# A retention layer followed by a low-rank mixer: stores moved to the GpSimd queue, and casts, transposes and scores placed as three separate steps

## The chip, the cores and the metric

The kernel runs on one core of one Trainium2 chip. The metric is the device time of a run in microseconds (us); of several runs the median counts. A core has five engines that run their own instruction streams in order and meet through semaphores: TensorE (PE in the profile, with PEld for its weight loads), VectorE (DVE), ScalarE (ACT), GpSimd (POOL) and SyncE (SP). A transfer is started by an instruction in the stream of one of these engines ("SPq", "ACTq" are the queues) and carried by 16 shared DMA engines.

## The reference

Four sequences (B = 4) of S = 768 tokens go through two layers. The first is a retention layer with H = 8 heads of D = 64: the state decays by a constant gamma of the head at each token and takes in the outer product of key and value, and the query reads it.

```python
for t in range(S):
    state = gamma * state + einsum('bhd,bhe->bhde', k[:, :, t], v[:, :, t])
    y[:, :, t] = scale * einsum('bhd,bhde->bhe', q[:, :, t], state)
```

Its output, laid out as x of shape (4, 768, 512), goes through a mixer: a low-rank mix over the tokens (rank 32), then a feed-forward part with 2048 hidden columns. Inputs and output are float32.

```python
h = xt @ U @ V                     # xt: x with tokens last
u = x + h.transpose(0, 2, 1)
out = u + maximum(u @ w_ch1, 0) @ w_ch2
```

## The kernel before

**Tiling.** A sequence is cut into six chunks of 128 tokens; two chunks make a block, so there are three blocks a sequence. In a chunk the retention is done in its parallel form: scores (key times query, masked to the causal half), a running state, and a mix of both into x.

**Steps of one block, and their lines.** `prep_block(b, bk)` (L205) is GpSimd work: it turns the loaded float32 tiles into bf16, `qTi` (L211, with the decay of the query), `kTi` (L215), and for each of the two chunks `kd` (L220) and `vd` (L225, with the decay of the key). After every one of these six casts it calls `feed_one` (L106), which puts the next load of a fixed list into SyncE's stream. `turn_block` (L327) makes VectorE transpose `qTi` and `kTi` in four instructions (L334). `score4(b, ci)` (L337) is the TensorE work of a chunk on the transposed tiles (L345), the causal mask on VectorE (L350), and the update of the state on TensorE (L363, which reads `kd` and `vd`), taken out of PSUM by ScalarE. `mix4` (L372) ends the chunk on TensorE (L382, L388), and ScalarE copies x out. When all six chunks are done, `lr_proj`, `lr_expand` and `lr_turn` (L400 to L431) do the low-rank mix and transpose its result u.

**The feed-forward part.** `mlp_pieces(b)` (L442) cuts it into 32 pieces "up" (16 with 512 columns, 16 with 256; four matmuls each on L451, then a Relu, every third on VectorE at L456 and the others on ScalarE at L458) and 24 pieces "down" (four matmuls each on L474; after each fourth piece VectorE adds u to the result in `o_sb`, L479, and a store of 256 KB is put on a list). Three buffers hold `o_sb`, so the add of the fourth tile needs the first store to have landed.

**What sets the order.** All streams are written by hand. `weave` (L488) writes the pieces of sequence b-1 one after the other, and between them, at given fractions of their total cost, the steps of sequence b: these are the marks, numbers in the tables `AT` (five for each block: begin, score, mix, score, mix) and `LR`. `store()` (L437) writes the next store of the list into ScalarE's stream, one piece after its add. In the table of before the first of the five marks of a block does both `prep_block` and `turn_block`. There are four weaves: in the first three the pieces of sequences 0, 1 and 2 run with the retention of sequences 1, 2 and 3 between them, and the fourth has the pieces of sequence 3 alone. Sequence 0's retention comes ahead of them, by a loop of its own, while the weights are loaded and cast.

**Buffers that the steps touch.** `rblk` has two buffers for each of `qTi`, `kTi` and the transposed `qT`, `kT`; `rpre` has four each for `kd` and `vd`, that is two blocks' worth; `rin2` has four for the loads of q and k in block form, again two blocks' worth; `rin` has 19 for all other loads. Each transfer that SyncE or ScalarE starts takes one of eight completion semaphores (DMAHW0 to DMAHW7), and waits until that semaphore's transfer before it has landed.

Of the kernel before, what the change touches and what calls it, by code (L numbers as in the profile page):

```python
# [17 lines left out]
def kernel(  # L18
# [11 lines left out]
    nc = tc.nc  # L30
    P = 128
    B, H, S, D = q.shape
# [73 lines left out]
    def feed_one():  # L106
        if n_fed[0] == len(feed):
            return
        key, src = feed[n_fed[0]]
        n_fed[0] += 1  # L110
        if key[0] == "uv":
            nc.sync.dma_start(out=Uf,
                              in_=moe_U.rearrange("(j p) r -> p j r", p=P))
            for c in range(NCB):
                nc.sync.dma_start(out=Vf[ds(RK * c, RK)], in_=moe_V)
            return
        if key[0] in ("qT", "kT"):
            t = rin2.tile([P, 1024], fp32, tag="in2", name=f"in2_{n_fed[0]}")
            ready[key] = t
            for hp in range(4):  # L120
                nc.sync.dma_start(
                    out=t[ds(32 * hp, 32)].rearrange("p (h x) -> p h x", h=2),
                    in_=src[ds(2 * hp, 2)].rearrange("h (t j) d -> t h (j d)",
                                                     t=32))
            return
        t = rin.tile([P, 512], fp32, tag="in", name=f"in_{n_fed[0]}")
        ready[key] = t
        if key[0] in "qkv":
            t = t.rearrange("p (h d) -> p h d", h=H)
        nc.sync.dma_start(out=t, in_=src)  # L130

    def take(*key):
        assert feed[n_used[0]][0] == key, (feed[n_used[0]][0], key)
        n_used[0] += 1
        return ready.pop(key, None)
# [69 lines left out]
    def prep_block(b, bk):  # L205
        for nm in ("qT", "kT"):
            src = take(nm, b, bk).rearrange("p (a j d) -> p a j d", a=8, j=2)
            t = rblk.tile([P, 8, D, 2], bf16, tag=nm + "i", name=f"{nm}i_{b}_{bk}")
            dst = t.rearrange("p a d j -> p a j d")
            if nm == "qT":  # L210
                nc.gpsimd.tensor_tensor(  # L211
                    dst, src, gqT[:, bk, :, :, None].to_broadcast([P, 8, 2, D]),
                    op=ALU.mult)
            else:
                nc.gpsimd.tensor_copy(out=dst, in_=src)  # L215
            pre[nm, b, bk] = t
            feed_one()
        for ci in (2 * bk, 2 * bk + 1):
            t = rpre.tile([P, H, D], bf16, tag="kd", name=f"kd_{b}_{ci}")
            nc.gpsimd.tensor_copy(  # L220
                out=t, in_=take("k", b, ci).rearrange("p (h d) -> p h d", h=H))
            pre["k", b, ci] = t
            feed_one()
            t = rpre.tile([P, H, D], bf16, tag="vd", name=f"vd_{b}_{ci}")
            nc.gpsimd.tensor_tensor(  # L225
                t, take("v", b, ci).rearrange("p (h d) -> p h d", h=H),
                gk[:, ci, :, None].to_broadcast([P, H, D]), op=ALU.mult)
            pre["v", b, ci] = t
            feed_one()
# [97 lines left out]
    def turn_block(b, bk):  # L327
        for nm in ("qT", "kT"):
            src = pre.pop((nm, b, bk)).bitcast(fp32).rearrange(
                "p (h j) (c w) o -> p h j c (w o)", h=2, c=2)  # L330
            t = rblk.tile([P, 2, 2, 256], bf16, tag=nm, name=f"{nm}_{b}_{bk}")
            dst = t.bitcast(fp32).rearrange("p h c (t j) -> p h j c t", j=4)
            for i in range(2):
                nc.vector.transpose(out=dst[:, i], in_=src[:, i])  # L334
            bts[nm, b, bk] = t
# [60 lines left out]
    def lr_open(b):  # L396
        us[b] = xp.tile([P, NCK, DM], bf16, tag="u", name=f"u_{b}")
        uTs[b] = xp.tile([P, NCB, S], bf16, tag="uT", name=f"uT_{b}")

    def lr_proj(b):  # L400
        for j in range(NCK):
            for c in range(NCB):
                nc.tensor.matmul(R[ds(RK * c, RK), 3, :P], Ub[:, j],  # L403
                                 xs[b][:, j, ts(c, P)], start=(j == 0),
                                 stop=(j == NCK - 1))
        pcs[b] = rmid.tile([P, P], bf16, tag="pc", name=f"pc_{b}")
        evac("D", pcs[b], R[:, 3, :P])
# [29 lines left out]
    def store():  # L437
        if stores:
            dst, src = stores.pop(0)
            nc.scalar.dma_start(out=dst, in_=src)  # L440

    def mlp_pieces(b):  # L442
        gT = gtp.tile([P, NM, S], bf16, tag="gT", name=f"gT_{b}")
# [44 lines left out]
    def weave(pieces, marks):  # L488
        total = sum(c for c, _ in pieces)
        marks = sorted(((total * at, f) for at, f in marks), key=lambda m: m[0])  # L490
        at = 0.0
        for cost, f in pieces:
            while marks and marks[0][0] <= at:
                marks.pop(0)[1]()
            late = len(stores)
            f()
            if late:
                store()
            at += cost
        for _, f in marks:  # L500
            f()
        while stores:
            store()

    def part(f, *args):
        return lambda: f(*args)
# [39 lines left out]
    for j in range(4):  # L546
        prep_w2(j)

    AT = {1: ((0.30, 0.33, 0.39, 0.43, 0.49), (0.62, 0.64, 0.69, 0.72, 0.77),
              (0.79, 0.81, 0.85, 0.87, 0.91)),  # L550
          2: ((0.12, 0.14, 0.20, 0.24, 0.30), (0.33, 0.35, 0.41, 0.45, 0.51),
              (0.54, 0.56, 0.62, 0.66, 0.72))}
    AT[3] = AT[2]
    LR = {1: (0.94, 0.96, 0.98, 0.99), 2: (0.76, 0.80, 0.88, 0.92)}
    LR[3] = LR[2]
    for b in range(1, B):
        if b > 1:
            marks = [(0.02, part(lr_expand, b - 1, 4, 2)),
                     (0.07, part(lr_turn, b - 1, 4))]
        else:  # L560
            marks = [(0.03, part(lr_expand, 0, 4, 2)), (0.10, part(lr_turn, 0, 4)),
                     (0.16, part(lr_expand, 0, 0, 4))]
        for bk in range(NBK):
            def begin(bk=bk):
                if (b, bk) != (1, 0):
                    prep_block(b, bk)
                turn_block(b, bk)
            ci = 2 * bk
            marks += zip(AT[b][bk], (begin, part(score4, b, ci), part(mix4, b, ci),
                                     part(score4, b, ci + 1),  # L570
                                     part(mix4, b, ci + 1)))

        def mixed():
            lr_open(b)
            lr_proj(b)
        marks += zip(LR[b], (mixed, part(lr_expand, b, 0, 4), part(lr_turn, b, 0),
                             part(lr_turn, b, 2)))
        weave(mlp_pieces(b - 1), marks)
    b = B - 1
# [32 lines left out]
```

## Time and profile before

| what | us |
|---|---|
| median of 3 runs (lowest to highest) | 267.06 (266.52 to 267.25) |
| the profiled execution, its own time | 268.16 |
| its span, first to last instruction | 266.3 |
| TensorE busy in the span | 226.4 |
| VectorE, ScalarE, GpSimd busy | 105.7, 84.0, 96.8 |
| mean granted TensorE clock | 0.974 |

The profiled execution's own time is 1.86 us longer than its span, and 1.10 us over the median. All views are of this execution, in us from the span's start. "Busy" of TensorE comes from modelled ends of its matmuls; what it lacks to the length of a stretch is time in which it waited.

### The profile page before, as it was taken

What the parts mean: (1) busy time and instruction counts of PE and PEld (TensorE: products, weight loads), DVE (VectorE), ACT (ScalarE), POOL (GpSimd) and SP (SyncE); (2) the same over time, 40 slices, a digit from 0 to 9 for tenths busy, and PEclk for the clock granted to TensorE, in tenths of its full rate; (3) what the DMA queues carried; (4) which work ended last, traced back from release to release, by engine and by line L of the source; (5) the groups of instructions that cost most, each with busy time, mean ns of one, the idle gap of its engine ahead of it and who ended that gap; (6) DMA issues with size and microseconds to landing.
All of it is one profiled execution on the core that took longest, in us unless ns stands there. A gap on an engine that the chain in (4) does not pass through costs nothing.

```text
span 266.3 us, 5538 instructions
## 1 busy us (share of the span) xinstructions
PE 226.4 (85%) x2284; PEld 123.8 (47%) x2284; DVE 105.7 (40%) x188; ACT 84.0 (32%) x159; POOL 96.8 (36%) x125
## 2 busy tenths in 40 slices
PE   1565557997997599497999999979999999999994
PEld 1344443445643234243575445435754454475441
DVE  3132212356352614236656333466563334232211
ACT  2533323444501010343553003435530034452000
POOL 4786584886503655455520242456000000000000
PEclk9999999999999859689999999999999999999999
DMA  8999899999319879599900675696002121000222
GB/s 165 218 218 192 271 382 194 279 380 234 76 50 260 206 195 237 142 190 219 221 6 2 153 210 172 163 240 116 0 5 81 42 79 39 0 2 0 79 81 79
DMA packets 70986, 39.14 MB, mean 147 GB/s; under 512 B 59056, under 2 KB 59056, under 8 KB 70960
## 3 DMA queue, kind: packets, MB, share of 16 engines
q1 hardware_dynamic: 67504, 32.48, 54.1%
q10 hardware_dynamic: 3456, 6.29, 6.4%
q8 instruction: 18, 0.29, 0.5%
q14 instruction: 8, 0.07, 0.1%
HBM read 32.47 MB, written 6.29 MB: 146 GB/s over the span
## 4 chain that ended last, share of the span: by engine, by line
PE 72%; DVE 6%; DMA 4%; ACT 2%; issue 1%; SPq 0%; POOL 0%; POOLq 0%; ACTq 0%; DVEq 0%
PE mlp L451 31%; PE mlp L474 30%; PE r L428 2%; PE r L345 2%; DMA in<-in_v_dram 2%; DVE qT L334 2%; DMA out_dram<-o 2%; PE r L388 2%; DVE kT L334 2%; DVE gT L456 1%; PE st L363 1%; ACT uT L76 1%; PE r L382 1%; PE r L412 1%; PE r L403 1%
## 5 line engine op out<-in xcount | busy, mean ns | idle before, releaser
L451 PE MATMUL mlp<-uT,w1b 128*128 128x512 bf16 (+1 forms) x512 | 92.0, 334 | 1.8 <-ACT uT L76 1.8
L474 PE MATMUL mlp<-w2b,gT 128*128 128x512 bf16 x384 | 90.5, 386 | 0.0
L451 PEld LDWEIGHTS <-w1b 128*128 128x128 bf16 x512 | 48.9, 99 | 34.8 <-issue 6.3
L458 ACT ACTIVATE gT<-mlp 128x512 bf16<-128x512 f32 (+1 forms) x88 | 42.8, 490 | 44.6 <-PE mlp L451 37.9
L474 PEld LDWEIGHTS <-gT 128*128 128x128 bf16 x384 | 36.0, 99 | 40.3 <-issue 2.2
L456 DVE TENSOR_SCALAR gT<-mlp 128x512 bf16<-128x512 f32 (+1 forms) x40 | 22.2, 555 | 39.9 <-PE mlp L451 39.9
L479 DVE TENSOR_TENSOR o<-mlp,u 128x512 f32<-128x512 f32 x24 | 16.5, 689 | 48.9 <-PE mlp L474 48.9
L350 DVE TENSOR_TENSOR a<-r,mask 128x512 bf16<-128x512 f32 x36 | 23.2, 685 | 15.3 <-PE r L345 9.9
L76 ACT ACTIVATE x<-r 128x512 bf16<-128x512 f32 x24 | 14.3, 596 | 38.5 <-PE r L388 32.4
L225 POOL TENSOR_TENSOR vd<-in,gk 128x512 bf16<-128x512 f32 x18 | 18.8, 1042 | 13.9 <-DMA in<-in_v_dram 8.9
L215 POOL CAST kTi<-in 128x1024 bf16<-128x1024 f32 x9 | 12.0, 1329 | 29.4 <-DMA in<-in_k_dram 25.5
L211 POOL TENSOR_TENSOR qTi<-in,gqT 128x1024 bf16<-128x1024 f32 x9 | 17.1, 1904 | 13.4 <-DMA in<-in_q_dram 9.3
L419 DVE TENSOR_TENSOR u<-r,x 128x512 bf16<-128x512 f32 (+1 forms) x16 | 14.6, 953 | 15.8 <-PE r L412 15.8
L303 DVE TENSOR_TENSOR a<-r,mask 128x512 bf16<-128x512 f32 x12 | 7.7, 686 | 26.2 <-ACT x L76 13.9
L76 ACT ACTIVATE uT<-r 128x1024 bf16<-128x1024 bf16 x10 | 10.2, 1021 | 24.9 <-PE r L428 24.9
L220 POOL CAST kd<-in 128x512 bf16<-128x512 f32 x18 | 11.0, 612 | 15.7 <-DMA in<-in_k_dram 15.2
L76 ACT ACTIVATE ns<-st 128x256 bf16<-128x256 f32 x15 | 5.7, 383 | 27.7 <-PE st L363 27.7
L345 PE MATMUL r<-qT,kT 32*128 32x128 bf16 x288 | 8.4, 218 | 6.3 <-DVE kT L334 6.3
L271 PE MATMUL r<-ident,qd 128*128 128x128 bf16 x24 | 3.5, 302 | 10.6 <-POOL qd L238 5.1
L76 ACT ACTIVATE qkT<-r 128x1024 bf16<-128x1024 bf16 x6 | 6.1, 1023 | 17.2 <-PE r L273 17.2
L252 POOL CAST w1b<-in 128x512 bf16<-128x512 f32 x16 | 9.8, 613 | 4.6 <-DMA in<-in_moe_w_ch_dram 4.0
L345 PEld LDWEIGHTS <-kT 32*128 32x128 bf16 x288 | 4.2, 92 | 14.3 <-DVE kT L334 10.2
(63 smaller groups left out, 148.5 us busy)
## 6 DMA issues: line engine op xcount, KB each, us to landing
in<-in_moe_w_ch_dram SPq DMA_DIRECT2D x32, 256.0 KB, 5.5
in<-in_k_dram SPq DMA_DIRECT2D x24, 256.0 KB, 5.0
in<-in_v_dram SPq DMA_DIRECT2D x24, 256.0 KB, 5.1
out_dram<-o ACTq DMA_DIRECT2D x24, 256.0 KB, 2.0
in<-in_q_dram SPq DMA_DIRECT2D x36, 128.0 KB, 4.7
in<-in_k_dram SPq DMA_DIRECT2D x36, 128.0 KB, 3.7
in<-in_q_dram SPq DMA_DIRECT2D x6, 256.0 KB, 5.1
Vf<-in_moe_V_dram SPq DMA_DIRECT2D x4, 96.0 KB, 3.9
```

The source lines that it names most:

```text
L76: nc.scalar.activation(dst, src, AF.Copy)
L211: nc.gpsimd.tensor_tensor(dst, src, gqT[:, bk, :, :, None].to_broadcast([P, 8, 2, D]), op=ALU.mult)
L215: nc.gpsimd.tensor_copy(out=dst, in_=src)
L225: nc.gpsimd.tensor_tensor(t, take("v", b, ci).rearrange("p (h d) -> p h d", h=H), gk[:, ci, :, None].to_broadcast([P, H, D]), op=ALU.mult)
L345: nc.tensor.matmul(R[:, hp, ts(i, P)], kT[r, i, c, tok], qT[r, i, c, tok], start=(c == 0), stop=(c == 1))
L350: nc.vector.tensor_tensor(a[:, ds(4 * g, 4)].rearrange("p (n i) m -> p n i m", n=2), R[:, ds(2 * g, 2), :256].rearrange("p n (i m) -> p n ...
L419: nc.vector.tensor_tensor(v4(us[b][:, ds(j0, nj), e]), R[:, ds(2 * g, 2), :nj * P].rearrange("p c (j e) -> p c j e", j=nj), v4(xs[b][:, ds ...
L451: nc.tensor.matmul(g_p[:, :sz], w1b[:, c, ts(m, P)], uTs[b][:, c, ds(lo, sz)], start=(c == 0), stop=(c == NCB - 1))
L456: nc.vector.tensor_relu(gT[:, m, ds(lo, sz)], g_p[:, :sz])
L458: nc.scalar.activation(gT[:, m, ds(lo, sz)], g_p[:, :sz], AF.Relu)
L474: nc.tensor.matmul(ch, gT[:, m, ts(j, P)], w2b[:, m], start=(m == 0), stop=(m == NM - 1))
L479: nc.vector.tensor_tensor(o_sb, ch, us[b][:, j], op=ALU.add)
```

## The change

Three things are edited.

1. `store()` issues the transfer from GpSimd's stream instead of ScalarE's.
2. `prep_block` is no longer part of a block's first mark. The casts of sequence 1's second block are written ahead of the first weave; the third block's casts of each sequence come right after the fifth mark of its first block, and the casts of the next sequence's first two blocks after the fifth marks of the second and third block. So every cast stands one block earlier than it did.
3. The marks are new numbers. A block's first mark, now the transposes alone, stands 0.05 to 0.07 of the pieces' cost ahead of the first score, where it was 0.02 or 0.03; and `lr_turn` moves from 0.07 to 0.06 in the second and third weave.

```diff
     def store():
         if stores:
             dst, src = stores.pop(0)
-            nc.scalar.dma_start(out=dst, in_=src)
+            nc.gpsimd.dma_start(out=dst, in_=src)
...
-    AT = {1: ((0.30, 0.33, 0.39, 0.43, 0.49), (0.62, 0.64, 0.69, 0.72, 0.77),
-              (0.79, 0.81, 0.85, 0.87, 0.91)),
+    prep_block(1, 1)
+
+    AT = {1: ((0.27, 0.32, 0.38, 0.42, 0.48), (0.56, 0.62, 0.67, 0.71, 0.76),
+              (0.74, 0.80, 0.84, 0.87, 0.91)),
...
-                     (0.07, part(lr_turn, b - 1, 4))]
+                     (0.06, part(lr_turn, b - 1, 4))]
...
-            def begin(bk=bk):
-                if (b, bk) != (1, 0):
-                    prep_block(b, bk)
-                turn_block(b, bk)
             ci = 2 * bk
-            marks += zip(AT[b][bk], (begin, part(score4, b, ci), part(mix4, b, ci),
-                                     part(score4, b, ci + 1),
+            marks += zip(AT[b][bk], (part(turn_block, b, bk), part(score4, b, ci),
+                                     part(mix4, b, ci), part(score4, b, ci + 1),
                                      part(mix4, b, ci + 1)))
+        marks.append((AT[b][0][4] + 0.005, part(prep_block, b, 2)))
+        if b + 1 < B:
+            marks.append((AT[b][1][4] + 0.005, part(prep_block, b + 1, 0)))
+            marks.append((AT[b][2][4] + 0.005, part(prep_block, b + 1, 1)))
```

**SyncE, the loads of sequence 1's second block.** The last four loads of that block (in_646 and in_649 are k and v of its second chunk) and what each waits for; DMAHW is the completion semaphore that it takes, Pool a buffer that GpSimd must have freed. Ahead of the change ScalarE's first store, of o_0, waits for and takes DMAHW6 too.

```order
-L130 DMA in_640<-in_k_dram 128x8x64 [waits DMAHW4_49,Pool_49]
-L130 DMA in_643<-in_v_dram 128x8x64 [waits DMAHW5_49,Pool_49]
-L130 DMA in_646<-in_k_dram 128x8x64 [waits DMAHW6_49,Pool_49]
-L130 DMA in_649<-in_v_dram 128x8x64 [waits DMAHW7_49,Pool_49]
+L130 DMA in_640<-in_k_dram 128x8x64 [waits DMAHW3_49,Pool_49]
+L130 DMA in_643<-in_v_dram 128x8x64 [waits DMAHW4_49,Pool_49]
+L130 DMA in_646<-in_k_dram 128x8x64 [waits DMAHW5_49,Pool_49]
+L130 DMA in_649<-in_v_dram 128x8x64 [waits DMAHW6_49,Pool_49]
```

With the stores gone from these eight semaphores, loads alone take them, strictly in turn, and each load waits for the load that stands eight ahead of it.

**GpSimd, the first weave.** What now stands between the casts of sequence 1's third block and those of sequence 2's first block; DMAHW are loads, PE buffers that TensorE must have read, and DVE in a store's row is the add that fills o_0, o_1 or o_2.

```order
L220 CAST kd_4_1086<-in_664 128x512 [waits DMAHW7_49,PE_49,Pool_49]
L225 TENSOR_TENSOR vd_4_1090<-in_667,gk 128x512 [waits DMAHW0_49,PE_49,Pool_49]
L220 CAST kd_5_1094<-in_670 128x512 [waits DMAHW1_49,PE_49,Pool_49]
L225 TENSOR_TENSOR vd_5_1098<-in_673,gk 128x512 [waits DMAHW2_49,PE_49,Pool_49]
L440 DMA out_dram<-o_0_1134 128x512 [waits DVE_49]
L440 DMA out_dram<-o_1_1191 128x512 [waits DVE_49]
L440 DMA out_dram<-o_2_1273 128x512 [waits DVE_49]
L211 TENSOR_TENSOR qTi_0_1312<-in_70_676,gqT 128x8x2x64 [waits DMAHW5_49,DMAHW4_49,DMAHW6_49,DMAHW3_49,Pool_49]
```

Before there were casts alone in this stream; now the first three stores stand behind the last cast of the third block, and the next block's casts behind the stores.

**VectorE, start of the second weave.** Before, from the first Relus (L456; mlp is a PSUM bank) to the mask of the first chunk's scores (L350):

```order
L456 TENSOR_SCALAR gT_1537<-mlp_1560 128x512
L456 TENSOR_SCALAR gT_1537<-mlp_1587 128x512
L334 STREAM_TRANSPOSE qT_0_1623<-qTi_0_1593 128x4x64 x2
L334 STREAM_TRANSPOSE kT_0_1626<-kTi_0_1600 128x4x64 x2
L350 TENSOR_TENSOR a_2_0_1651<-r,mask 128x512 x2
```

And with the change, the same stretch:

```order
L456 TENSOR_SCALAR gT_1597<-mlp_1620 128x512
L334 STREAM_TRANSPOSE qT_0_1641<-qTi_0_1312 128x4x64 x2
L334 STREAM_TRANSPOSE kT_0_1644<-kTi_0_1319 128x4x64 x2
L456 TENSOR_SCALAR gT_1597<-mlp_1653 128x512
L350 TENSOR_TENSOR a_2_0_1681<-r,mask 128x512 x2
```

The four transposes moved ahead of the second Relu, which follows a matmul group three pieces later in TensorE's stream.

More of the change, by code (lines that the diff above doesn't have):

```diff
@@ L547 @@
         prep_w2(j)
-    AT = {1: ((0.30, 0.33, 0.39, 0.43, 0.49), (0.62, 0.64, 0.69, 0.72, 0.77),
-              (0.79, 0.81, 0.85, 0.87, 0.91)),
-          2: ((0.12, 0.14, 0.20, 0.24, 0.30), (0.33, 0.35, 0.41, 0.45, 0.51),
-              (0.54, 0.56, 0.62, 0.66, 0.72))}
+    prep_block(1, 1)
+    AT = {1: ((0.27, 0.32, 0.38, 0.42, 0.48), (0.56, 0.62, 0.67, 0.71, 0.76),
+              (0.74, 0.80, 0.84, 0.87, 0.91)),
+          2: ((0.08, 0.13, 0.19, 0.23, 0.29), (0.27, 0.34, 0.40, 0.44, 0.50),
+              (0.48, 0.55, 0.61, 0.65, 0.71))}
     AT[3] = AT[2]
```

## The prediction

> **What bounds it now.** The first rows are from the page: the busy line, and the shares of the chain that ended last.
>
> ```profile
> PE 226.4 (85%) x2284; PEld 123.8 (47%) x2284; DVE 105.7 (40%) x188; ACT 84.0 (32%) x159; POOL 96.8 (36%) x125
> PE 72%; DVE 6%; DMA 4%; ACT 2%; issue 1%; SPq 0%; POOL 0%; POOLq 0%; ACTq 0%; DVEq 0%
> ```
>
> TensorE bounds the kernel and nothing else comes near, so a change gains only what TensorE loses by waiting or by a low clock. Next I cut the span into its weaves: the chain in order of time (start, length, what) has the first matmuls of each.
>
> ```profile
> 43.90 3.57 PE mlp L451 x8
> 111.64 1.87 PE mlp L451 x4
> 166.90 0.86 PE mlp L451 x4
> 220.13 0.86 PE mlp L451 x4
> ```
>
> The three weaves that carry retention work take 67.7, 55.3 and 53.2 us for nearly the same matmuls, so the losses sit in the first. The view of windows finds them (length, then busy us of PE, PEld, DVE, ACT, POOL; granted clock; DMA share; GB/s).
>
> ```profile
> 58.00:62.00 4.00, 2.77 (x13) 1.08 (x11) 2.10 (x6) 1.79 (x3) 3.50 (x6) 1.00 1.05 339
> 62.00:66.00 4.00, 3.68 (x65) 3.08 (x66) 2.60 (x6) 1.64 (x5) 1.82 (x4) 1.00 0.84 201
> 70.00:74.00 4.00, 4.00 (x47) 2.37 (x46) 0.74 (x2) 1.60 (x4) 0.81 (x1) 1.00 0.02 4
> 94.00:96.00 2.00, 2.00 (x6) 0.74 (x5) 0.69 (x1) 0.00 (x0) 0.79 (x1) 0.50 1.03 243
> 120.00:122.00 2.00, 0.62 (x11) 0.12 (x9) 2.00 (x5) 0.60 (x1) 1.09 (x2) 1.00 1.07 227
> 122.00:124.00 2.00, 1.83 (x38) 0.90 (x31) 1.53 (x3) 0.52 (x2) 0.85 (x1) 1.00 1.06 227
> 170.00:180.00 10.00, 8.46 (x82) 4.12 (x80) 5.13 (x9) 4.76 (x9) 4.95 (x5) 1.00 0.93 221
> ```
>
> At each first block TensorE stands still for 1.5 us; near 95 us it is busy at half clock; and at 70 to 74 us the DMA engines carry nothing (share 0.02). The timeline of TensorE shows what the pauses between 82 and 94 us waited for (in brackets), and those of SyncE and ScalarE why.
>
> ```profile
> 85.09 0.30 PE L363 MATMUL st<-vd,kd 128*32 128x64 bf16 x16 [1.98 <-POOL vd L225]
> 90.68 0.29 PE L345 MATMUL r<-qT,kT 32*128 32x128 bf16 x8 [1.16 <-DVE kT L334]
> 91.14 0.29 PE L345 MATMUL r<-qT,kT 32*128 32x128 bf16 x8 [0.17 <-DVE kT L334]
> 92.99 0.41 PE L363 MATMUL st<-vd,kd 128*32 128x64 bf16 x16 [1.56 <-POOL vd L225]
> 65.48 0.53 SPq L130 DMA_DIRECT2D in<-in_v_dram  x1
> 78.31 0.37 SPq L130 DMA_DIRECT2D in<-in_k_dram  x1
> 76.19 0.37 ACTq L440 DMA_DIRECT2D out_dram<-o  x1
> ```
>
> SyncE issues a load of v at 65.48 and nothing more until 78.31, 2.1 us after ScalarE issued the first store: that k load takes the semaphore which the store had. From there everything is late: loads, GpSimd's casts, VectorE's transposes, TensorE.
>
> **The change part by part.** *Stores off the eight semaphores, casts a block early.* SyncE's next load no longer waits for a store, so it can go at 66.0 instead of 78.3: the third block's loads, and with them its casts, move up by 12.3 us. GpSimd's timeline has those casts, the page their means.
>
> ```profile
> 81.49 0.61 POOL L220 CAST kd<-in 128x512 bf16<-128x512 f32 x1 [10.67 <-DMA in<-in_k_dram]
> 91.89 1.04 POOL L225 TENSOR_TENSOR vd<-in,gk 128x512 bf16<-128x512 f32 x1 [1.42 <-DMA in<-in_v_dram]
> 93.75 1.04 POOL L225 TENSOR_TENSOR vd<-in,gk 128x512 bf16<-128x512 f32 x1
> L211 POOL TENSOR_TENSOR qTi<-in,gqT 128x1024 bf16<-128x1024 f32 x9 | 17.1, 1904 | 13.4 <-DMA in<-in_q_dram 9.3
> L215 POOL CAST kTi<-in 128x1024 bf16<-128x1024 f32 x9 | 12.0, 1329 | 29.4 <-DMA in<-in_k_dram 25.5
> ```
>
> The chunk whose `vd` came at 91.89 then has it at 79.6 to 80.6; TensorE reaches it at 90.68 less the pauses ahead (1.55 + 1.98 + 1.16), 86.0. Some 5 us of cover: the four pauses of 1.98, 1.16, 0.17 and 1.56 us go, **4.87 us**. The pause at the first block, 1.23 + 0.32 = **1.55 us**, goes by the transposes (below).
>
> *The half clock.* It follows the pauses; with them it should go. The chain shows equal groups of L474 at both clocks.
>
> ```profile
> 93.39 3.53 PE mlp L474 x8
> 97.79 1.34 PE mlp L474 x4
> 101.86 1.73 PE mlp L474 x8
> 104.04 0.97 PE mlp L474 x4
> ```
>
> That is 1.80 + 0.37 = **2.17 us** (small matmuls between left out).
>
> *Transposes ahead of the score.* In the second weave the chain has a Relu, four transposes, then the score.
>
> ```profile
> 119.68 0.69 DVE gT L456
> 120.37 1.00 DVE qT L334 x2
> 121.36 0.92 DVE kT L334 x2
> 113.97 1.29 DVE L419 TENSOR_TENSOR u<-r,x 128x512 bf16<-128x512 f32 x2 [5.62 <-PE r L412]
> ```
>
> Before, one piece (four matmuls, 0.86 us) stood between mark and score, against 0.69 + 1.92 = 2.61 us of VectorE. Now three pieces (2.6 us) stand there and that Relu is behind the transposes, so 1.92 is covered. The casts they read are a block old. Gains: 1.38 + 0.17 = **1.55 us** in the second weave, 10.00 - 8.46 = **1.54 us** in the third.
>
> *`lr_turn` one piece earlier.* It waits for adds of 1.29 us (last row above, timeline of VectorE); two pieces, 1.73 us, are left in front. I take 0; at worst it waits out the piece it passed, 0.86 us in two weaves, 1.7 us.
>
> *What GpSimd now holds.* A block costs 1.90 + 1.33 + 2 x (0.61 + 1.04) = 6.53 us, three blocks, as the first two weaves have, 19.6 us of some 51.7 (53.2 less the pause). Six stores come on top. Their price on this engine is not in the trace: from 0.37 us (ScalarE's issue) to 5.5 (the slowest median landing below, were the engine held that long); I take 1.04, that of `vd`, a GpSimd instruction over a tile of that shape. Queued behind a waiting store are casts needed a block later, hidden by that block; behind a waiting cast are stores, and for them VectorE's add waits.
>
> ```profile
> 95.25 0.69 DVE L479 TENSOR_TENSOR o<-mlp,u 128x512 f32<-128x512 f32 x1 [2.43 <-PE mlp L474]
> 262.46 0.69 DVE L479 TENSOR_TENSOR o<-mlp,u 128x512 f32<-128x512 f32 x1 [2.76 <-PE mlp L474]
> 263.19 0.34 ACTq L440 DMA_DIRECT2D out_dram<-o  x1
> out_dram<-o ACTq DMA_DIRECT2D x24, 256.0 KB, 2.0
> in<-in_moe_w_ch_dram SPq DMA_DIRECT2D x32, 256.0 KB, 5.5
> ```
>
> The tightest place: store o_0 stands behind the `vd` of 93.75, done at 94.79 - 12.3 = 82.5; with 1.04 of issue and 2.0 of landing it is out at 85.5. The add that reuses its buffer was at 95.25; less the pauses ahead of it (1.55 + 4.87) and about half of the slow clock's loss (estimated 1), 87.8. Some 2 us of margin; the next mask follows some 3 us later, so TensorE feels it only beyond 5.
>
> *The last store* has no cover: issue at 263.19, 2.0 to land. From GpSimd, 1.04 of issue for 0.34: **0.7 us lost**; bounds 0 and, with a landing of 5.5 for 2.0, 0.7 + 3.5 = 4.2.
>
> The Trainium skill ("DMA: Bandwidth & Descriptors", Latency and other measured facts) puts the first byte at about 1 us from GpSimd against 0.6 us from ScalarE; no store of this trace goes by GpSimd. By its figures the loss would be 0.4 us (an estimate) and the forecast 255.7.
>
> **Sum**: 1.55 + 4.87 + 2.17 + 1.55 + 1.54 = 11.68 gained, 0.7 lost: 11.0 us. From the profiled execution's 268.16: 257.2. The median before is 1.1 lower, 267.06, which gives **256.0**.
>
> **The rivals.** *A part stays* (0.23). The loads move up but are bound by the DMA engines (share 0.84 to 1.07 when they flow), or VectorE is late for another reason. If the later weaves' 3.1 us remain: 259.1. If half of the first weave's 4.87 comes back and the clock falls with it, 2.4 + 2.2: 260.6. For it: margins of 2 and 5 us are worked out from a shift, not seen. Against: the idle DMA engines at 70 to 74 us.
>
> *The second slow stretch goes too* (0.08). At the end of the first weave TensorE waits again and falls to half clock; this row of the chain above, 1.87 for four matmuls instead of 0.97, is part of it.
>
> ```profile
> 107.81 0.61 PE L428 MATMUL r<-ident,u 128*128 128x128 bf16 x8 [1.49 <-DVE u L419]
> 109.52 1.01 PE L428 MATMUL r<-ident,u 128*128 128x128 bf16 x8 [1.11 <-ACT uT L76]
> ```
>
> These waits are a chain of the low-rank steps whose order stays, so I leave them in. If the clock held there, some 2 us more would go: 254.
>
> *GpSimd becomes the bound: slower* (0.06). If a store held GpSimd for P us, it would need 19.6 + 6P in each of the first two weaves; their 51.7 us are reached at P = 5.35, and the gain of 11 us is eaten from 2 x (19.6 + 6P - 51.7) = 11, P = 6.3. At P = 7 the time is 256.0 + 2 x 9.9 = 276. The place would be the adds at L479 waiting for a buffer. No cast takes longer than 1.90, so P would have to be of a landing's size.
>
> *A store waits for VectorE* is a smaller mechanism for P, counted under "a part stays". If a store could not be issued until VectorE's instruction under way has ended, at worst the pair of adds of 1.29, P would be 1.04 + 1.29 = 2.3 and o_0 out at 86.8: still ahead of the add at 87.8, and the last store follows VectorE's last instruction. It stays at 256.
>
> The Trainium skill ("SBUF — State Buffer", SBUF: two separate sides) speaks against the change in this way: GpSimd cannot write a transfer's descriptors while VectorE runs a two-port operation, and it advises ScalarE or SyncE for the transfer. No run here shows such a wait so far.
>
> *It doesn't do what it says* (0.03). If the k load at 66 waited for something else until 78, only the transposes' 3.1 us (and the first 1.55) would come: 267.06 - 4.65 + 0.7 = 263.1.
>
> **How the numbers follow.** Forecast 256.0 with chance 0.60; its own range is 253.5 to 258. Adding the partial rival and the clock's brings 0.91; the case that does nothing for the loads is faster too. The end's bound of 4.2 and `lr_turn`'s 1.7 push the top by up to 5.2: 261.2. The range 252.5 to 262 holds all but the slower rival and stray cases. A measurement of this kernel tells 0.3% (0.8 us) from no change. Faster 0.89, being 0.94 less 0.05 for gains eaten by an end and a GpSimd cost near their upper bounds; same 0.04 of those; slower 0.07, the rest of them and the rival.
>
> **What would show it.** Right: SyncE issues on at 66 us without the 12 us hole; no wait for `vd` at L363; no wait for `kT` at L345; clock 1.00 from 90 to 100 us; the first weave near 59 us, the second and third near 53.7 and 51.7; the span's end at most 1 us further behind the last add than the 3.15 us of now. Wrong: adds at L479 waiting for a transfer, GpSimd's store instructions over 2 us, or new waits of TensorE on VectorE near 86 us.

## The result and the profile after

| what | before | after |
|---|---|---|
| median in one session, us (lowest to highest, 4 runs each) | 266.79 (266.24 to 267.25) | 254.9 (254.58 to 256.46) |
| ratio, with its 95% interval | | 0.9567 [0.9523, 0.9611] |
| the profiled execution's own time, us | 268.16 | 256.46 |
| its span, us | 266.3 | 254.6 |
| mean granted TensorE clock | 0.974 | 0.985 |
| GpSimd busy, us | 96.8 | 109.5 |

The change makes the kernel 11.9 us faster by the medians and 11.7 us by the two profiled executions; the forecast was 11.0. On the page of after the busy line reads:

```profile
PE 219.8 (86%) x2257; PEld 122.9 (48%) x2284; DVE 105.9 (42%) x188; ACT 84.5 (33%) x159; POOL 109.5 (43%) x149
```

TensorE still bounds the kernel. The timeline of after (start, length, what; in brackets the idle time ahead of a row and what ended it) has the first matmuls of the four weaves, the last add and the last store:

```profile
44.04 2.29 PE L451 MATMUL mlp<-uT,w1b 128*128 128x512 bf16 x5 [0.68 <-ACT uT L76]
...
102.61 1.87 PE L451 MATMUL mlp<-uT,w1b 128*128 128x512 bf16 x4 [1.11 <-ACT uT L76]
...
155.79 1.03 PE L451 MATMUL mlp<-uT,w1b 128*128 128x512 bf16 x4
...
207.03 1.03 PE L451 MATMUL mlp<-uT,w1b 128*128 128x512 bf16 x4
...
249.53 0.69 DVE L479 TENSOR_TENSOR o<-mlp,u 128x512 f32<-128x512 f32 x1 [2.76 <-PE mlp L474]
250.52 0.54 POOL L440 DMA_DIRECT2D out_dram<-o  x1 [2.92 <-DVE o L479]
```

The same rows of before start at 43.90, 111.64, 166.74 and 219.97; the last two of them are

```profile
166.74 1.03 PE L451 MATMUL mlp<-uT,w1b 128*128 128x512 bf16 x4
219.97 1.03 PE L451 MATMUL mlp<-uT,w1b 128*128 128x512 bf16 x4
```

and its last add ends at 263.15. That gives the lengths:

| stretch, us | before | after | difference | forecast |
|---|---|---|---|---|
| first weave | 67.74 | 58.57 | -9.17 | -8.59 |
| second weave | 55.10 | 53.18 | -1.92 | -1.55 |
| third weave | 53.23 | 51.24 | -1.99 | -1.54 |
| fourth weave, to the end of the last add | 43.18 | 43.19 | +0.01 | 0 |
| last add to the end of the span | 3.15 | 4.38 | +1.23 | +0.7 |

Where the time came from is best read in the view of waits, cut to the three weaves (44 to 215 us): who waited for whom, us in total, times, the longest. Before:

```profile
PE r L345 <- DVE kT L334: 6.3, 10, 1.4
PE st L363 <- POOL vd L225: 3.5, 2, 2.0
PE mlp L451 <- ACT uT L76: 1.8, 2, 1.1
PE r L428 <- DVE u L419: 1.5, 1, 1.5
PE r L428 <- ACT uT L76: 1.1, 1, 1.1
```

After:

```profile
PE mlp L451 <- ACT uT L76: 1.8, 2, 1.1
PE mlp L474 <- issue: 1.6, 10, 0.2
PE r L428 <- DVE u L419: 1.5, 1, 1.5
PE r L428 <- ACT uT L76: 1.1, 1, 1.1
```

The waits for `kT` and `vd`, 9.8 us, are gone to the last one; the three waits of the low-rank tail stand there unchanged. Most of the rest is the clock. In windows of before (columns as in the prediction: length, busy PE, PEld, DVE, ACT, POOL, granted clock, DMA share, GB/s) there are two long stretches at half clock:

```profile
92.00:98.50 6.50, 5.51 (x51) 2.29 (x51) 1.51 (x3) 0.98 (x2) 4.45 (x4) 0.50 0.76 190
99.00:108.50 9.50, 7.92 (x113) 3.82 (x113) 5.22 (x7) 0.65 (x2) 4.49 (x5) 1.00 0.93 231
109.00:115.50 6.50, 4.87 (x25) 2.00 (x25) 1.29 (x2) 2.09 (x3) 2.15 (x2) 0.50 0.28 88
```

Of after, one is left, behind the tail's waits, and the place that idled at 70 to 74 us now loads:

```profile
70.00:74.00 4.00, 4.00 (x37) 2.19 (x29) 1.81 (x4) 1.12 (x3) 2.26 (x4) 1.00 0.99 197
94.00:99.50 5.50, 3.72 (x58) 1.83 (x58) 3.24 (x4) 0.09 (x1) 3.48 (x4) 1.00 1.03 266
100.00:106.50 6.50, 4.57 (x24) 2.05 (x25) 1.29 (x2) 2.06 (x3) 5.02 (x7) 0.50 1.13 231
```

In the lost stretch TensorE was busy 5.51 of 6.5 us at half clock, so it lost about half of that, 2.8 us. That is an estimate. With the 9.8 us of waits it gives 12.6 of the 13.1 us by which the three weaves became shorter (9.17 + 1.92 + 1.99).

SyncE's timeline shows the loads that had stood still from 65.5 to 78.3 us:

```profile
64.95 1.42 SPq L130 DMA_DIRECT2D in<-in_v_dram  x1
66.46 1.52 SPq L130 DMA_DIRECT2D in<-in_k_dram  x1
68.07 0.96 SPq L130 DMA_DIRECT2D in<-in_v_dram  x1
69.09 4.09 SPq L121 DMA_DIRECT2D in<-in_q_dram  x4
```

Most of the signs that the prediction named are there: SyncE issues on, no wait for `vd` or `kT` is left, the clock stays at 1.00 up to 99.9 us, and the weaves have the lengths that it gave, to 0.5 us. Two are not as it said. The end is 1.23 us longer, where it allowed at most 1; and one sign of being wrong showed up, an add at L479 that waits 1.45 us for a transfer, though TensorE did not feel it (both below). What the result alone cannot tell is which of the three edits brought the gain: the experiments take them apart.

### The profile page after: what moved, and what is told of

Read it like the earlier page. It is cut to its first block, busy times and chain, and to the rows that moved or that the text cites. A ratio compares the mean times of both kernels' runs of the same rounds, so it can differ in the third digit from the quotient of the medians.

```text
span 254.6 us, 5508 instructions
## 1 busy us (share of the span) xinstructions
PE 219.8 (86%) x2257; PEld 122.9 (48%) x2284; DVE 105.9 (42%) x188; ACT 84.5 (33%) x159; POOL 109.5 (43%) x149
## 4 chain that ended last, share of the span: by engine, by line
PE 48%; issue 30%; POOL 3%; DVE 2%; ACT 2%; POOLq 0%; ACTq 0%; DVEq 0%
PE mlp L451 22%; PE mlp L474 15%; POOL out_dram L440 2%; PE r L345 2%; PE r L388 2%; PE r L428 2%; PE st L363 1%; ACT uT L76 1%; PE r L382 1%; PE r L412 1%; PE r L403 1%; DVE a L303 1%; DVE u L419 1%; DVE a L350 1%; ACT x L76 0%
## 5 line engine op out<-in xcount | busy, mean ns | idle before, releaser
L451 PE MATMUL mlp<-uT,w1b 128*128 128x256 bf16 (+1 forms) x503 | 91.5, 333 | 3.1 <-ACT uT L76 1.8
L474 PE MATMUL mlp<-w2b,gT 128*128 128x512 bf16 x366 | 85.4, 379 | 2.0 <-issue 1.6
L440 POOL DMA_DIRECT2D out_dram<-o x24 | 13.3, 556 | 87.2 <-DVE o L479 87.2
L456 DVE TENSOR_SCALAR gT<-mlp 128x512 bf16<-128x512 f32 (+1 forms) x40 | 22.3, 557 | 33.4 <-PE mlp L451 33.3
L479 DVE TENSOR_TENSOR o<-mlp,u 128x512 f32<-128x512 f32 x24 | 16.5, 689 | 44.7 <-PE mlp L474 43.2
L350 DVE TENSOR_TENSOR a<-r,mask 128x512 bf16<-128x512 f32 x36 | 23.1, 684 | 14.4 <-PE r L345 13.5
L258 POOL CAST w2b<-in 128x512 bf16<-128x512 f32 x16 | 9.7, 616 | 2.2 <-DMA in<-in_moe_w_ch_dram 1.5
## 6 DMA issues: line engine op xcount, KB each, us to landing
in<-in_moe_w_ch_dram SPq DMA_DIRECT2D x32, 256.0 KB, 5.4
in<-in_k_dram SPq DMA_DIRECT2D x24, 256.0 KB, 5.1
in<-in_v_dram SPq DMA_DIRECT2D x24, 256.0 KB, 5.5
out_dram<-o POOLq DMA_DIRECT2D x24, 256.0 KB, 2.3
in<-in_q_dram SPq DMA_DIRECT2D x6, 256.0 KB, 5.2
```

Source lines behind the costliest of these rows:

```text
L350: nc.vector.tensor_tensor(a[:, ds(4 * g, 4)].rearrange("p (n i) m -> p n i m", n=2), R[:, ds(2 * g, 2), :256].rearrange("p n (i m) -> p n ...
L440: nc.gpsimd.dma_start(out=dst, in_=src)
L451: nc.tensor.matmul(g_p[:, :sz], w1b[:, c, ts(m, P)], uTs[b][:, c, ds(lo, sz)], start=(c == 0), stop=(c == NCB - 1))
L456: nc.vector.tensor_relu(gT[:, m, ds(lo, sz)], g_p[:, :sz])
L474: nc.tensor.matmul(ch, gT[:, m, ts(j, P)], w2b[:, m], start=(m == 0), stop=(m == NM - 1))
L479: nc.vector.tensor_tensor(o_sb, ch, us[b][:, j], op=ALU.add)
```

## The experiments

Each run is compared with runs of the kernel before on the same chip; the medians of those were 267.11 us (e1 to e4), 267.41 (e5 to e8) and 266.92 (e9, e10).

### The store queue alone (e1)

The kernel before, with this edit and nothing else:

```diff
-            nc.scalar.dma_start(out=dst, in_=src)
+            nc.gpsimd.dma_start(out=dst, in_=src)
```

> The kernel before with one edit: stores from GpSimd. Theory T (the gain comes from loads that no longer wait for a store's semaphore, and needs the casts written a block early, because a store in GpSimd's stream holds the casts behind it): SyncE's hole at 66 to 78 us is gone, but store o_0, whose add ends at 76, now stands ahead of the casts of sequence 1's second block and store o_2 ahead of the third block's, so TensorE waits some 3 us at each for kT and vd, the clock falls again, and the last store costs 1.2 more: 267 to 271 us, no faster than before. Rival R1 (the stores alone bring the first weave's gain): 267 - 7 + 1.2 = 261 us.

Measured: 272.41 us (271.27 to 273.56), ratio 1.0199 [1.0152, 1.0245]: **slower**, though not surely by 2%, and a little above the 267 to 271 us of theory T. The hole in SyncE's stream is gone (it issues a k load at 65.00), yet TensorE waits longer than before. GpSimd's timeline says why, and TensorE's what follows:

```profile
77.54 0.71 POOL L440 DMA_DIRECT2D out_dram<-o  x1 [13.40 <-DVE o L479]
78.27 1.92 POOL L211 TENSOR_TENSOR qTi<-in,gqT 128x1024 bf16<-128x1024 f32 x1
...
82.17 0.29 PE L345 MATMUL r<-qT,kT 32*128 32x128 bf16 x8 [3.09 <-DVE kT L334]
...
96.23 0.29 PE L345 MATMUL r<-qT,kT 32*128 32x128 bf16 x8 [2.41 <-DVE kT L334]
```

GpSimd stood 13.40 us in front of the first store, until VectorE's add filled o_0, and the block's casts, whose loads were long there, stood behind it. The waits for `kT` come to 10.8 us, against 9.8 for `kT` and `vd` before. Of the 5.4 us of span (266.3 to 271.7), the first weave takes 2.6, the third 1.7 (a stretch at half clock fell into it) and the end 1.2; of the first weave's loss 1.0 is in these waits and 0.9 lies ahead of its first score, which comes 19.15 us behind the weave's first matmul (63.22 less 44.07) where it came 18.26 before (62.16 less 43.90); why that is, and the remaining 0.7, is open. So the wait moved from a semaphore to a queue, and the early casts are what the store's move to GpSimd needs, not a gain beside it: with them, at the same marks, the time is 263.44 (e3).

### Stores back on ScalarE, the rest of the change kept (e2)

```diff
-            nc.gpsimd.dma_start(out=dst, in_=src)
+            nc.scalar.dma_start(out=dst, in_=src)
```

> The changed kernel with one edit undone: stores from ScalarE. Theory T: SyncE again waits for store o_0, but by the order of the instructions the load that takes its semaphore is now one of k of the third block, seven loads later in the stream than before, so the hole begins near 71 us and ends near 77; vd of the fifth chunk is cast near 87 instead of 80.4, close to TensorE's need at 86: 0 to 3 us lost there, and the last store gains 1.2: 254 to 257 us. Rival R2 (it is the queue of the stores that removes the 7 us of the first weave): 254.9 + 7 - 1.2 = 261 us.

Measured: 256.0 us (255.92 to 257.12), ratio 0.9597 [0.9557, 0.9638]. That is nearly the whole gain, without the new queue. It is also without the early casts: with the stores out of GpSimd's stream that stream holds casts alone, and SyncE's loads alone, so casts written a block earlier stand in the same order as before, on every engine, and every load takes the same semaphore as it would with the casts in their old places. This run is thus **the marks alone**; and early casts alone, with the old marks and ScalarE's queue, would be the kernel before, instruction for instruction. SyncE's timeline still shows loads that wait for stores, but others and later:

```profile
70.62 7.94 SPq L121 DMA_DIRECT2D in<-in_k_dram  x4
81.46 0.38 SPq L130 DMA_DIRECT2D in<-in_k_dram  x1
```

With the new marks the steps reach the load list in another place among the stores: the load that takes the first store's semaphore is now seven loads further down. Of the waits for `kT` and `vd` TensorE keeps one, as the timeline and the view of waits show it:

```profile
88.24 0.30 PE L363 MATMUL st<-vd,kd 128*32 128x64 bf16 x16 [1.45 <-POOL vd L225]
PE st L363 <- POOL vd L225: 1.5, 1, 1.5
```

The half clock is down to one stretch of 3.4 us.

### The old marks under the new queue and the early casts (e3)

The changed kernel with the `AT` rows of before and `lr_turn` at 0.07.

> The changed kernel with the marks of before (tables AT and lr_turn's 0.07), casts and stores as changed. Theory T: the pauses of 1.5 us at the first block of each of three weaves come back, for VectorE has one piece for a Relu and four transposes: 254.9 + 1.55 + 1.55 + 1.54 = 259.5 us. Rival R3 (with casts a block early the transposes are ready anyway and the marks do nothing): 255 us.

Measured: 263.44 us (262.25 to 264.14), ratio 0.9858 [0.9818, 0.9898]. Both guesses were off. The view of waits of this run, over the same stretch as above, starts with:

```profile
PE r L345 <- DVE kT L334: 5.0, 8, 1.4
PE mlp L451 <- ACT uT L76: 1.8, 2, 1.1
```

No wait for `vd` is left, but the pauses for `kT` at the first block of each weave, 4.64 us in the prediction, are all there (5.0 us with two of 0.17 at second blocks). Without the marks the two other edits bring 3.7 us, where 6.34 (4.87 + 2.17 - 0.7) had been put down to it. A part of that difference has a place in the trace: the tail's stretch at half clock now lies over busy work.

```profile
103.50:110.00 6.50, 5.59 (x20) 1.88 (x21) 1.45 (x3) 1.72 (x3) 1.81 (x3) 0.50 1.13 269
```

TensorE is busy 5.59 of these 6.5 us, where it was 4.57 of 6.5 in the changed kernel's stretch; at half clock that is worth 0.5 us. The end is longer too, 4.42 us behind the last add where 3.15 + 0.7 had been reckoned. The rest of the difference was not traced.

### No store in the first weave, else the kernel before (e4)

```diff
-    def weave(pieces, marks):
+    def weave(pieces, marks, no_stores=False):
...
+            if no_stores:
+                stores.clear()
+                late = 0
...
-        weave(mlp_pieces(b - 1), marks)
+        weave(mlp_pieces(b - 1), marks, b == 1)
```

> The kernel before with the six stores of the first weave left out (the output of sequence 0 is not written), everything else as before: no store stands between the loads of sequence 1's second and third block. Theory T: the hole of SyncE at 66 us is gone and with it the pauses at vd and kT of the second and third block and the half clock after them: 267 - 4.87 - 2.17 = 260 us. Rival R4 (the loads wait for buffers or for the DMA engines, not for a store): 267 us, with the hole still there.

The output of sequence 0 is missing in this kernel. Measured: 261.42 us (260.23 to 263.19), ratio 0.9792 [0.9733, 0.9851]. SyncE issues on where it stood still before, and the waits at the first weave's second and third block are gone; the 5.0 us of waits for `kT` stay, to the tenth those of e3:

```profile
65.28 2.38 SPq L130 DMA_DIRECT2D in<-in_k_dram  x1
PE r L345 <- DVE kT L334: 5.0, 8, 1.4
```

So the **store in the shared semaphore is what made the hole**. Without it the time falls by 5.7 us under the old marks (267.11 to 261.42; 4.0 to 7.1 by the interval). That holds the traffic of six stores as well, which this run leaves out. e3, which closes the hole with all stores kept, gains 3.7, and there the end takes 1.3 us more than in before (4.42 against 3.15).

### The change once more (e5)

> The changed kernel once more, as the reference for the three below and beside the stores-from-ScalarE run. All theories: 254.9 us, 254.5 to 256.5 by how long the slow clock at the end of the first weave lasts.

Measured: 255.63 us (254.78 to 256.74), ratio 0.9557 [0.9526, 0.9589]. Against e2's 0.9597 [0.9557, 0.9638] the intervals overlap: by the ratios the new queue with its casts is worth about 1 us on top of the marks, and not surely that.

### The last six stores from ScalarE (e6), and each store cut in two (e7)

e6 is the changed kernel with

```diff
-                    stores.append((out[b, ts(j, P)], o_sb))
+                    stores.append((out[b, ts(j, P)], o_sb,
+                                   nc.scalar if b == B - 1 else nc.gpsimd))
```

> The changed kernel, but the six stores of the last sequence go out from ScalarE again. Theory T (a store from GpSimd costs more only where nothing covers it, at the end: 4.38 us from the last add to the span's end against 3.15): 254.9 - 1.2 = 253.7 us. Rival R5 (the longer end is not the store's queue but the time the engines take to close): 254.9.

e7 issues each store of the changed kernel as two halves of 128 KB:

```diff
-            nc.gpsimd.dma_start(out=dst, in_=src)
+            for i in range(2):
+                nc.gpsimd.dma_start(out=dst[:, ds(256 * i, 256)],
+                                    in_=src[:, ds(256 * i, 256)])
```

> The changed kernel with every store cut into two of half the columns, so GpSimd issues 48 transfers instead of 24: 24 x 0.54 = 13 us more on that engine. Theory T (GpSimd has slack in every weave, and VectorE's add may wait for a buffer without TensorE feeling it): at most 0.6 more at the end, 254.9 to 255.6 us. Rival R6 (GpSimd's share is near a bound, the queue behind the stores delays casts): 258 us or more, with TensorE waiting for vd or kT.

Measured, e6: 254.64 us (253.75 to 255.59), ratio 0.952 [0.9487, 0.9553]; the last add ends at 250.10 and the span at 253.5, so the end takes 3.40 us where it took 4.42 in e5 beside it. By the medians e6 is 1.0 us below e5, as theory T had it, with intervals that just overlap. Against e2's 0.9597 [0.9557, 0.9638] it is 2 us better: under these marks queue and casts do gain something in the weaves, 1.45 of it the pause for `vd` that e2 keeps, and in the changed kernel the longer end takes back about half. Measured, e7: 257.19 us (256.69 to 258.4), ratio 0.9619 [0.9586, 0.9652], and all that it lost against e5 is at the end (the two added lines shift the numbers of those behind them):

```profile
248.46 0.69 DVE L481 TENSOR_TENSOR o<-mlp,u 128x512 f32<-128x512 f32 x1 [2.76 <-PE mlp L476]
249.44 1.07 POOL L441 DMA_DIRECT2D out_dram<-o  x2 [2.38 <-DVE o L481]
```

The add ends at 249.15 and the span at 255.3: 6.15 us. What takes so long is a drain: the instruction that closes GpSimd's stream behind its last store. The rows of the closing line, in before, after and e7 (duration in ns, shortest, middle and longest; first and last start in us):

```profile
L607 POOLq DRAIN  x3: 40/78/1142, 184.7 to 266.0; - x3
L609 POOLq DRAIN  x3: 40/102/3327, 250.5 to 254.3; - x3
L611 POOLq DRAIN  x3: 40/102/4641, 249.9 to 255.0; - x3
```

The first of the three is the longest. With all stores from GpSimd it starts with the last of them and lasts 3.33 us in after, to 253.8, and 4.64 in e7, to 254.5; either span ends 0.8 us behind it. In before it was over long before the end. Why it is longer behind twice the issues is open. In the weaves the six more issues a sequence cost nothing: no wait for `vd` or `kT` came back, so the time lies between theory T's 255.6 and rival R6's 258 by the end alone.

### The tail's waits (e8, e9) and the queue under better marks (e10)

e8 takes e6 and moves the third block of the first weave and the low-rank steps behind it forward:

```diff
-              (0.74, 0.80, 0.84, 0.87, 0.91)),
+              (0.71, 0.77, 0.81, 0.84, 0.88)),
...
-    LR = {1: (0.94, 0.96, 0.98, 0.99), 2: (0.76, 0.80, 0.88, 0.92)}
+    LR = {1: (0.90, 0.92, 0.96, 0.98), 2: (0.76, 0.80, 0.88, 0.92)}
```

> The changed kernel with the last sequence's stores from ScalarE and, in the first weave, the third block's five marks 0.03 earlier and the four low-rank marks at 0.90, 0.92, 0.96, 0.98 instead of 0.94, 0.96, 0.98, 0.99. Theory T (the waits of 1.49, 1.11 and 1.11 us at the end of the first weave come from low-rank steps with too few pieces between them, and the slow clock follows from these waits): some 2.4 us of the waits and the 2.2 us of the slow clock go: 253.7 - 4.6 = 249 us, clock 1.00 there. Rival R7 (the slow clock comes at that place whatever the waits): 251.3 us, with the clock at 0.50 for 3.4 us or more. Rival R8 (the third block's loads are late for marks 0.03 earlier): a new wait for vd at L363, 253 us or more.

Measured: 252.11 us (251.53 to 252.33), ratio 0.9422 [0.9395, 0.9448]. The waits of the tail fell from 3.71 to 1.99 us only, and one of 0.69 us came where a score now stands straight behind a mix, but the clock stayed up (mean 1.000), so rival R7 is out. The time is 2.5 us below e6 where theory T had 4.6, for the waits did not all go. The place that ran at half clock in after:

```profile
100.00:106.50 6.50, 5.33 (x39) 2.54 (x38) 3.49 (x7) 3.76 (x6) 4.16 (x6) 1.00 1.15 228
```

e9 spaces these marks better, with a piece between that mix and that score and one behind the last `lr_turn`; e10 is e9 with all 24 stores from ScalarE.

```diff
-    AT = {1: ((0.27, 0.32, 0.38, 0.42, 0.48), (0.56, 0.62, 0.67, 0.71, 0.76),
-              (0.71, 0.77, 0.81, 0.84, 0.88)),
+    AT = {1: ((0.27, 0.32, 0.38, 0.42, 0.48), (0.54, 0.60, 0.65, 0.69, 0.74),
+              (0.69, 0.77, 0.80, 0.83, 0.87)),
...
-    LR = {1: (0.90, 0.92, 0.96, 0.98), 2: (0.76, 0.80, 0.88, 0.92)}
+    LR = {1: (0.895, 0.915, 0.95, 0.975), 2: (0.76, 0.80, 0.88, 0.92)}
```

> Theory: what e8 left of TensorE's waits at the end of the first weave (0.63 + 0.25 + 1.11 us, and 0.69 us before the score that stands straight behind a mix) is only spacing. Here a piece stands between that mix and that score, and one piece between the last lr_turn and the start of the second weave, so 0.69 and about 1.0 of the 1.11 go: 252.1 - 1.7 = 250.4 us, no stretch at half clock. Rival: the chain of low-rank steps and the retention's masks are bounded by VectorE and ScalarE, so that the waits only move to other places of the block: 252 us, as e8.

> The same marks as e9, with all 24 stores from ScalarE as in the kernel before. Theory: the marks carry the gain and the store queue does not, so this is within 1 us of e9 (250.4, in a range of 249.5 to 251.5), the end a little shorter or equal. Rival: with the marks of the third block some 2 us earlier, the loads that wait for the first store (a hole of about 8 us in SyncE's stream) come too late for the casts; TensorE then waits 2 to 4 us for vd and kT at the third block, as in the kernel before, and the clock falls again: 253 to 256 us.

Measured: e9 250.77 us (250.33 to 252.18), ratio 0.9399 [0.9365, 0.9432]; e10 250.4 us (249.97 to 250.77), ratio 0.9382 [0.9353, 0.9412]. Both theories held: 16 us off the kernel before, 4 to 5 off the changed one, and the queue of the stores makes no difference that this measurement can tell. The profiled run of e9, its slowest, has one wait that e10 lacks, on VectorE and from there on TensorE (whether e9's faster runs have it too, no trace shows):

```profile
89.86 0.69 DVE L479 TENSOR_TENSOR o<-mlp,u 128x512 f32<-128x512 f32 x1 [4.00 <-DMA out_dram<-o]
90.47 1.28 DVE L350 TENSOR_TENSOR a<-r,mask 128x512 bf16<-128x512 f32 x2
...
91.80 0.30 PE L382 MATMUL r<-ns,qT 32*128 32x64 bf16 x16 [1.69 <-DVE a L350]
```

This is the prediction's tightest place: the add of o_3 waits for store o_0, which GpSimd issues at 84.34 behind the third block's casts, and ScalarE in e10 at 75.26. With ScalarE the price is on the load side, and is covered there: the cast of `kTi` waits 4.03 us for its load, and TensorE does not feel it.

## Why the prediction was right, and where its reasons were not

The time and the sum held, and most of the signs; the shares of the edits did not. The total is also nearer than its parts: the weaves gave 13.1 us where 11.7 had been summed, and the end took 1.23 where 0.7 had.

**The pauses: right.** 9.51 us of them were to go (4.87 + 1.55 + 1.55 + 1.54) and 9.8 went. Each was named with its place, and none stayed. The 0.3 us between the two sums are waits for `kT` of 0.16 and 0.17 us at the second block of the second and third weave (133.50 and 186.73 us in before), which the prediction left out.

**Which edit takes them: wrong for the larger part.** "*Stores off the eight semaphores, casts a block early*" was given 4.87 us of pauses and 2.17 of clock. The mechanism is real (e4: without the stores there is no hole), but the step took it that only the queue's move could close it. The new marks alone shift which load meets the first store's semaphore, and leave 1.45 us of those pauses (e2). Nothing in the prediction saw that: two edits of the change each take most of the same pauses, so that the total alone could not show this step to be wrong. And the queue's move alone puts the casts behind the stores and loses 5.3 us (e1); the rival "GpSimd becomes the bound" looked for this loss in the price of a store, and it was in the wait ahead of one. Both edits were read from one trace, in which either would do; what they are worth is not a sum: 3.7 us (e3) and 11.1 us (e2) alone, 11.9 together.

**The half clock: right in kind, too small.** 2.17 us came from two groups of matmuls; the whole stretch, 6.8 us with TensorE busy for 5.5 of 6.5, is worth some 2.8 (an estimate: half of the busy time). Its size hangs on what lies under the stretch, as e3 shows from the other side.

**Transposes ahead of the score: right.** 1.55 and 1.54 us forecast in the second and third weave, 1.92 and 1.99 measured; e3, which has the old marks, keeps just these waits. Of the rest, some 0.4 us each, 0.16 and 0.17 are the waits at the second block named above; 0.2 to 0.3 each was not traced. `lr_turn` one piece earlier cost nothing: no new wait at L428 stands in the table.

**The store's price: too high, and its wait too low.** The taken 1.04 us was 0.54 (539 to 709 ns, 24 instructions), so the rival in which GpSimd becomes the bound at 6.3 us was far off. But store o_0 went out only at 84.34, since the `vd` ahead of it waited for a load until 83.35, and the add that waits for its landing started 5.1 us later, where 2.0 had been taken for a landing, the median of before. That add came at 89.46, where 87.8 had been forecast, so the margin of 2 us was not there. (The step also counted an issue twice, 0.34 us: a landing is counted from the start of its issue.)

```profile
89.46 0.69 DVE L479 TENSOR_TENSOR o<-mlp,u 128x512 f32<-128x512 f32 x1 [1.45 <-DMA out_dram<-o]
```

The second slack, the 3 us to the next mask, held: TensorE did not feel it, as the prediction had it; in e9, where the marks are tighter, it did.

**The last store: 0.7 forecast, 1.23 measured**, inside the bounds of 0 and 4.2. The step took the issue alone, 0.7 us longer; it is 0.20 longer (0.54 for 0.34). Counted from the start of the issue, and with it, a landing takes 0.3 longer (2.3 for 2.0 in the middle). The instruction starts 0.30 us after the add's end (250.52 against 250.22), where ScalarE's started 0.04 after it (263.19 against 263.15). That makes 0.56. The other 0.67 lie behind the landing, 1.78 us to the end of the span against 1.11 before, and there stands GpSimd's drain (shown with e7), for which the sum had no term. From ScalarE (e6) 1.02 of the loss comes back.

By the first-byte figures of the Trainium skill ("DMA: Bandwidth & Descriptors", Latency and other measured facts) the loss had been estimated at 0.4 us; the trace has three times that. The Trainium skill ("SBUF — State Buffer", SBUF: two separate sides) warns that VectorE's two-port work holds up GpSimd's descriptors; the longest of the 24 issues took 0.71 us, with VectorE busy for 42% of the span, so no issue here shows such a hold; whether any of VectorE's instructions beside them was of that kind, the trace does not say.

**The second slow stretch** was left in, with a chance of 0.08 that it goes, and it stayed. That its waits are a chain whose order stays was true of this change; e8 and e9 show that marks set them too.

## What to carry to other kernels

Before giving a gain to one edit of several, ask of each wait that goes which of the edits would remove it alone, and what each edit does to the order of every queue: an edit that moves work in a stream that holds nothing else does nothing. A transfer that waits for a result belongs on a queue where nothing urgent stands behind it, and it takes a completion semaphore that other transfers may have to wait for; both prices are to be read from the rows ahead of the first store. Where a wait of TensorE of one or two us is followed by a lower clock, spacing the steps can bring more than the wait itself: from e6 to e8 TensorE's waits fell by 1.0 us net (1.72 less the new 0.69), and the time by 2.5. And a queue that carries the last transfer of a kernel has its closing on the clock: here GpSimd's drain.

## What the runs showed of the hardware

The half clock comes in stretches of about 3.4 or 6.8 us and nothing between: 6.8 twice before (91.9 to 98.6 and 108.8 to 115.6, read in windows of 0.5 us), 6.8 once in after, 3.4 once in e2, 3.4 four times in e1, 6.8 and 3.4 in e4, none in e8 (in e9 one sets in within the last us of the span, where the trace ends). In after it sets in at 99.9, between a wait of TensorE of 1.49 us that ended at 98.77 and the end of one of 1.11 at 100.48, and it stays away where the same places wait 0.63, 0.25 and 1.11 us (e8). In the 3.4 us ahead of that start TensorE waited 2.1 us in all; ahead of the first stretch of before it waited 1.8. At which share the clock falls, no run here shows. The Trainium skill ("TensorE: Matmul & The Clock Gate", What's actually happening) gives a free-running window of 3413 ns, which these lengths agree with. Its rule that the clock falls after an idle window of about 3.4 us does not fit here: the longest wait ahead of the stretch in after is 1.49 us.

An issue from GpSimd took 0.54 us for 256 KB, and two of 128 KB took 1.07: the price is that of the instruction, not of the bytes. Behind GpSimd's last store its drain took 3.33 us (4.64 with the stores cut in two), and the kernel's end waited for it; with the last six stores on ScalarE (e6) the drain starts at 208.1 us and is covered.
